# A two-part sequence kernel: constant tables and a channel kernel loaded early, a 127-partition load split, and a second inverse transform in full width

## The chip, the cores and the metric

The kernel runs on one core of one Trainium2 chip. The metric is device time in microseconds (us) of one execution. Engines are called as in the profile: PE (matmul), PEld (weight load), DVE (VectorE), ACT (ScalarE), POOL (GpSimd), SP (SyncE, which here only issues transfers). A suffix q, as in SPq, is the sequencer of an engine. L123 is a line of the kernel in question; the two kernels number their lines differently. "Slow" executions are those that the records mark by a lower granted clock or a time over 1.5% above the fastest of the same kernel; only fast ones are compared. The granted clock is PE's clock as the chip's throttle allowed it, as a share of full speed; the DMA share is the mean busy share of the 16 engines that carry out the core's transfers.

## The reference

Two heads are computed from separate inputs and concatenated. Head A is a diagonal state-space recurrence over 2048 steps with 640 complex states; head B multiplies a short shifted convolution of k by v, convolves the product along the sequence with a 2048-tap kernel for each channel (by FFT), and gates with q.

```python
# A: x [1, 2048, 640]
Lam_bar = exp(dt * Lam);  B_bar = ((Lam_bar - 1) / Lam)[:, None] * Bmat
h_t = Lam_bar * h_{t-1} + B_bar @ x_t
y_A = 2 * real(h @ Cmat.T) + x * Dskip
# B: q, k, v [1, 2048, 640]
kv  = (sum over t of shift(k, t) * shift_k[:, t]) * v
y_B = q * (causal_conv(kv, ssm_k) + kv * ssm_D)
out = concatenate([y_A, y_B], -1)          # bfloat16
```

## The kernel before

Head A first has a setup: B and C are loaded and transposed on PE, x is transposed by the transfer engines, sine and cosine tables are built on DVE, and C is scaled by complex factors. Then, for 20 tiles, come matmuls with B (`st_bu`), a rotation on DVE (`st_rot_in`), a scan and a rotation back (`st_scan`), and later the projection with C.

Head B has four phases, spread over A's steps: `ker` transforms the convolution kernel, `sig` forms kv on DVE and transforms it, `spec` multiplies the spectra, and `inv` goes back and gates with q. They communicate through scratch tensors in DRAM (`scr_ker`, `scr_sig`, `scr_inv`). Every `scr_inv` tile needs all of `ker` and `sig`, and the `inv` phase needs all of `spec`. A framework lays the tiles out in memory like a stack of pools and decides the order of instructions on each engine; that order is fixed when the program is built, so an engine that waits for one input cannot turn to the next instruction.

The parts that the change touches:

```python
# A's setup: everything here lives in pools that close at its end ... [cut]
for src, nm in ((A_C_re, "Cre"), (A_C_im, "Cim")):
    nat[nm] = setup.tile([P, NPT, D], B16, name=f"{nm}_nat")
    nc.sync.dma_start(nat[nm][:], ...)
t1 = setup.tile([P, NPT, NA, NB], F32); t2 = ...        # 2560 elements a partition
nc.vector.tensor_mul(t1[:], bca(CA), bcb(CB))           # six such products in all
...
# B, opened only after A's setup is closed: fp32 tables, staged and cast
with tc.tile_pool(name="b_cstage", bufs=2) as cst:
    self._cast_table(cst, "F1", F1np, self.F1sb, nc.scalar)      # 2 x 1 MB fp32, ACT casts
    ... S2, I2: load, cast;  sk_raw: load, ACT copies into skt
# then the stream pools, then ksb (2.5 MB), in memory that setup or the staging used
...
# sig: the three rows ahead of the tile come from the partition below
nc.sync.dma_start(kh[:, 3 - j0:JC + 3, :], self.k_v[:, 0:j0 + JC, :])
nc.sync.dma_start(kh[1:P, 0:3 - j0, :], self.k_v[0:P - 1, NJ - 3 + j0:NJ, :])   # 127 partitions
...
# spec: the product of half h goes through its own 64-column matmul at once
y_sb = self.sw.tile([P, 512], B16, name="y_sb")
nc.vector.tensor_mul(y_sb[:, 0:cw], pg[:, 0:cw], kt_sb[:, 0:cw])
if h == 0:
    st[("bps", ci)] = self.psum.tile([P, 512], F32, name="bank")
bps = st[("bps", ci)]
nc.tensor.matmul(bps[64*h:64*h+64, lo:hi], lhsT=self.I2sb[:, ..., :], rhs=y_sb[:, lo:hi],
                 start=True, stop=True, tile_position=(0, 64 * h))
if h == 1:
    nc.scalar.copy(Bf[:, c0:c0 + cw], bps[:, 0:cw])
```

## Time and profile before

The median of the first four runs is 366.4 us (363.98 to 368.54). Busy times over the span of 366.8 us:

| engine | busy us | share |
|---|---|---|
| DVE | 281.0 | 77% |
| PE | 237.1 | 65% |
| ACT | 189.8 | 52% |
| POOL | 9.8 | 3% |

I cut the span at three instructions: the first rotation of A (end of setup), the first spectral product y_sb, and the end of the last h_im (end of the spectrum stage). This is the table of busy times by stretch of the kernel before, cut there; the columns are stretch, length, then busy us (and instructions) of PE, PEld, DVE, ACT, POOL, the granted clock, the DMA share and GB/s.

```profile
0.00:48.93 48.93, 15.50 (x120) 12.13 (x120) 34.12 (x92) 25.86 (x46) 4.85 (x10) 0.91 0.65 128
48.93:192.48 143.55, 81.92 (x430) 40.81 (x431) 116.79 (x251) 79.13 (x152) 4.93 (x7) 0.76 0.61 211
192.48:324.29 131.81, 111.09 (x527) 43.06 (x527) 117.38 (x252) 80.09 (x168) 0.00 (x0) 0.95 0.34 117
324.29:366.80 42.51, 28.64 (x204) 17.93 (x202) 12.68 (x25) 4.70 (x12) 0.00 (x0) 0.89 0.77 259
```

Length less DVE's busy time is called DVE's hole in the stage: 26.8 us between setup and spectrum stage, and 14.4 us in the spectrum stage.

### The profile page before, as it was taken

The numbers are of one execution on the slowest core, as the hardware profiler recorded it, in microseconds if no ns is written. First come the engines' busy times: TensorE is split into PE (matmuls) and PEld (weight loads), VectorE is DVE, ScalarE is ACT, GpSimd is POOL, SyncE is SP. The second block draws the span as 40 slices with busy tenths as digits, with TensorE's granted clock in tenths as the row PEclk, the third lists the DMA queues.
The fourth block names the chain that finished last, engine by engine and source line by source line (L and its number), as shares of the span: only waits on it lengthen the run. The fifth ranks groups of instructions, "written<-read, shape, count | busy, mean of one in ns | idle before, by whom it ended". The sixth has DMA issues, their size and how long they took to land.

```text
span 366.8 us, 4211 instructions
## 1 busy us (share of the span) xinstructions
PE 237.1 (65%) x1279; PEld 113.9 (31%) x1279; DVE 281.0 (77%) x616; ACT 189.8 (52%) x377; POOL 9.8 (3%) x17
## 2 busy tenths in 40 slices
PE   2309100680468665673978878879988979786963
PEld 2207000530133222341632424232422424254532
DVE  0399998250589999999999999998898795933333
ACT  1188704770569674565546464747567574730000
POOL 5000020200000000000000000000000000000000
PEclk9999655687559986985898999998989998999888
DMA  7992059440569978853503333333344433147995
GB/s 218 119 236 109 0 170 385 160 160 28 209 183 362 327 243 301 273 184 106 183 32 108 127 108 126 112 122 113 121 155 138 157 109 126 37 165 224 324 324 182
DMA packets 42966, 62.93 MB, mean 172 GB/s; under 512 B 13090, under 2 KB 32161, under 8 KB 42432
## 3 DMA queue, kind: packets, MB, share of 16 engines
q1 hardware_dynamic: 30864, 40.76, 37.7%
q10 hardware_dynamic: 11552, 20.45, 14.5%
q0 software_dynamic: 528, 1.45, 1.5%
q8 instruction: 10, 0.16, 0.2%
q14 instruction: 12, 0.10, 0.1%
HBM read 39.06 MB, written 20.97 MB: 164 GB/s over the span
## 4 chain that ended last, share of the span: by engine, by line
DVE 45%; PE 22%; DMA 20%; issue 5%; SPq 4%; ACT 3%; POOL 1%; DVEq 0%; ACTq 0%; POOLq 0%
DMA in<-in_B_k_dram 6%; PE bank L600 6%; DVE y_sb L595 5%; DMA out_dram<-o 5%; DVE w L535 5%; PE bank L581 5%; DVE g_im L361 4%; DMA cstage<-b_F_d 4%; PE bank L582 3%; DVE g_re L360 3%; DMA dsk_raw<-in_A_Dskip_dram 3%; SPq L517 3%; PE bank L389 2%; DVE o L647 2%; PE bank L321 2%
## 5 line engine op out<-in xcount | busy, mean ns | idle before, releaser
L588 ACT CAST kt_sb<-bank 128x512 bf16<-128x512 f32 (+1 forms) x96 | 47.5, 521 | 22.0 <-PE bank L581 21.2
L595 DVE TENSOR_TENSOR y_sb<-bank,kt_sb 128x512 bf16<-128x512 f32 (+1 forms) x96 | 54.0, 594 | 5.7 <-ACT kt_sb L588 3.1
L490 ACT CAST o<-bank 128x512 bf16<-128x512 f32 x64 | 36.2, 602 | 34.3 <-PE bank L488 13.4
L600 PE MATMUL bank<-y_sb,b_I 128*64 128x512 bf16 (+2 forms) x97 | 34.3, 382 | 23.3 <-DVE y_sb L595 22.6
L389 PE MATMUL bank<-CtRe,h_re 128*128 128x320 bf16 x160 | 48.2, 319 | 0.0
L391 PE MATMUL bank<-CtImN,h_im 128*128 128x320 bf16 x160 | 47.7, 317 | 0.0
L535 DVE TENSOR_TENSOR w<-in,skt 128x1280 bf16<-128x1280 bf16 x32 | 25.2, 815 | 25.9 <-DMA in<-in_B_k_dram 25.9
L402 ACT CAST o_sb<-bank 128x320 bf16<-128x320 f32 x32 | 13.6, 426 | 55.2 <-PE bank L398 55.2
L581 PE MATMUL bank<-in,b_S 128*128 128x512 bf16 (+2 forms) x97 | 35.0, 362 | 0.0
L582 PE MATMUL bank<-in,b_S 128*128 128x512 bf16 (+2 forms) x97 | 34.4, 356 | 0.0
L647 DVE TENSOR_TENSOR o<-bank,in 128x512 bf16<-128x512 f32 x16 | 10.3, 683 | 26.6 <-DMA out_dram<-o 19.2
L603 ACT CAST o<-bank 128x512 bf16<-128x512 f32 (+1 forms) x48 | 24.7, 516 | 9.8 <-PE bank L600 9.2
L321 PE MATMUL bank<-xT,BreT 128*128 128x512 bf16 x100 | 29.4, 431 | 0.2
L488 PE MATMUL bank<-w,b_F 128*128 128x512 bf16 x32 | 14.0, 491 | 21.1 <-DVE w L541 18.6
L323 PE MATMUL bank<-xT,BimT 128*128 128x512 bf16 x100 | 26.1, 393 | 0.0
L504 PE MATMUL bank<-identb,ksb 128*128 128x128 bf16 x80 | 6.6, 248 | 29.1 <-POOL ksb L476 29.1
L581 PEld LDWEIGHTS <-b_S 128*128 128x128 bf16 x97 | 9.4, 97 | 43.1 <-issue 38.5
L488 PE MATMUL bank<-in,b_F 128*128 128x512 bf16 x32 | 12.8, 437 | 11.8 <-ACT o L490 10.2
L389 PEld LDWEIGHTS <-h_re 128*128 128x128 bf16 x160 | 16.7, 104 | 10.1 <-issue 3.6
L360 DVE TENSOR_TENSOR_SCAN g_re<-r,carry_re,mA 128x512 bf16<-128x512 f32 x15 | 19.1, 1274 | 0.0
L361 DVE TENSOR_TENSOR_SCAN g_im<-r,carry_im,mC 128x512 bf16<-128x512 f32 x15 | 19.0, 1269 | 0.0
L391 PEld LDWEIGHTS <-h_im 128*128 128x128 bf16 x160 | 16.6, 104 | 6.7 <-issue 0.5
(161 smaller groups left out, 420.3 us busy)
## 6 DMA issues: line engine op xcount, KB each, us to landing
scr_ker<-o ACTq DMA_DIRECT2D x16, 320.0 KB, 5.3
scr_sig<-o ACTq DMA_DIRECT2D x16, 320.0 KB, 3.1
in<-scr_ker SPq DMA_DIRECT2D x16, 320.0 KB, 2.8
in<-scr_sig SPq DMA_DIRECT2D x16, 320.0 KB, 3.4
scr_inv<-o ACTq DMA_DIRECT2D x16, 320.0 KB, 2.7
in<-scr_inv SPq DMA_DIRECT2D x16, 320.0 KB, 5.6
in<-in_B_k_dram SPq DMA_DIRECT2D x6, 800.0 KB, 6.2
ksb<-in_B_ssm_k_dram SPq DMA_DIRECT2D x1, 2560.0 KB, 17.6
```

Source lines behind the costliest of these rows:

```text
L321: nc.tensor.matmul(a_ps[:, 0:T], lhsT=self.BreT[:, kt, psl], rhs=self.xT[:, kt, tsl], start=(kt == 0), stop=(kt == NPT - 1))
L360: nc.vector.tensor_tensor_scan(g_re[:], rb, u_re[:], init_re, op0=ALU.mult, op1=ALU.add)
L361: nc.vector.tensor_tensor_scan(g_im[:], rb, u_im[:], init_im, op0=ALU.mult, op1=ALU.add)
L389: nc.tensor.matmul(o_ap, lhsT=h_re[:, pt, tt * P:(tt + 1) * P], rhs=self.CtRe[:, pt, half * H:(half + 1) * H], start=first, stop=False)
L391: nc.tensor.matmul(o_ap, lhsT=h_im[:, pt, tt * P:(tt + 1) * P], rhs=self.CtImN[:, pt, half * H:(half + 1) * H], start=False, stop=False)
L490: nc.scalar.copy(a2[:, u, 0:W0], main[:, 0:W0])
L535: nc.vector.tensor_mul(t[:], kh[:, 3 - i:JC + 3 - i, :], skb(i))
L581: nc.tensor.matmul(pk[:, lo:hi], lhsT=self.S2sb[:, 5 if sp else 2 + h, :], rhs=A1["ker"][:, c0 + lo:c0 + hi], start=True, stop=True)
L582: nc.tensor.matmul(pg[:, lo:hi], lhsT=self.S2sb[:, 4 if sp else 0 + h, :], rhs=A1["sig"][:, c0 + lo:c0 + hi], start=True, stop=True)
L588: nc.scalar.copy(kt_sb[:, 0:cw], st[x][0][:, 0:cw])
L595: nc.vector.tensor_mul(y_sb[:, 0:cw], pg[:, 0:cw], kt_sb[:, 0:cw])
L600: nc.tensor.matmul(bps[64 * h:64 * h + 64, lo:hi], lhsT=self.I2sb[:, 1 if sp else 0, :], rhs=y_sb[:, lo:hi], start=True, stop=True, tile_p ...
```

## The change

Its intent is to get the start-up out of the way. Tables come as bf16 and go straight to where they stay; tables and ksb get memory of their own, apart from setup's, so that their loads can start at once; to make room, setup uses less memory (two rotating buffers for B and C, the sine tables by state tile). The 127-partition load is split into 112 and 15. The second inverse transform becomes two accumulating matmuls of 128 columns, both issued after the second half's product.

```diff
@@ A's setup
-                nat[nm] = setup.tile([P, NPT, D], B16, name=f"{nm}_nat")
+                nat[nm] = natp.tile([P, NPT, D], B16, name="nat")      # natp: bufs=2
...              # C is loaded inside pe_transpose, still on nc.sync
-            t1 = setup.tile(shp, F32, name="tab_t1"); ...              # [P, NPT, NA, NB], 6 products
+            for pt in range(NPT):                                      # [P, NA, NB], 30 products
+                t1 = tmp.tile(shp, F32, name="tab_t1"); ...
@@ B's tables: no staging, no cast
-            self._cast_table(cst, "F1", F1np, self.F1sb, nc.scalar)
+        for nm, arr, dst, eng in (("F1", F1np, self.F1sb, nc.scalar), ("S2", ..., nc.gpsimd), ("I2", ..., nc.gpsimd)):
+            self._load_table(nm, arr, dst, eng)                        # one load into dst
@@ ksb
-        knat = ctx.enter_context(tc.tile_pool(name="bk_nat", bufs=1))
+        knat = self.const
@@ sig
-            nc.sync.dma_start(kh[1:P, 0:3 - j0, :], self.k_v[0:P - 1, NJ - 3 + j0:NJ, :])
+            nc.sync.dma_start(kh[1:113, 0:3 - j0, :], self.k_v[0:112, NJ - 3 + j0:NJ, :])
+            nc.sync.dma_start(kh[113:P, 0:3 - j0, :], self.k_v[112:P - 1, NJ - 3 + j0:NJ, :])
@@ spec
-            y_sb = self.sw.tile([P, 512], B16, name="y_sb")
+            y_sb = self.sw.tile([P, 512], B16, name=f"y_sb{h}")
             if h == 0:
-                st[("bps", ci)] = self.psum.tile([P, 512], F32, name="bank")
...
+                st[("y0", ci)] = y_sb
+                return
+            bps = self.psum.tile([P, 512], F32, name="bank")
+            nc.tensor.matmul(bps[:, lo:hi], lhsT=self.I2sb[:, ..., :], rhs=y0[:, lo:hi], start=True, stop=False)
+            nc.tensor.matmul(bps[:, lo:hi], lhsT=self.I2sb[:, ..., :], rhs=y_sb[:, lo:hi], start=False, stop=True)
@@ main: constants of B are allocated before A's setup runs, stream pools after it
```

More of the change, by code (lines that the diff above doesn't have):

```diff
@@ L133, in _sbuf_tables @@
     Minv, Minv0 = _is2_tables()
-    I2bd = np.zeros((128, 2, 64))
-    for gi in range(2):
-        rs = slice(64 * gi, 64 * gi + 64); cs = slice(32 * gi, 32 * gi + 32)
-        I2bd[rs, 0, cs] = Minv
-        I2bd[rs, 1, cs] = Minv0 if gi == 0 else Minv
+    I2bd = np.zeros((128, 2, 2, 128))
+    for v in range(2):
+        for h in range(2):
+            for gi in range(2):
+                g = 2 * h + gi
+                rs = slice(64 * gi, 64 * gi + 64); cs = slice(32 * g, 32 * g + 32)
+                I2bd[rs, v, h, cs] = Minv0 if (v == 1 and g == 0) else Minv
+    I2bd = I2bd.reshape(128, 4, 128)
     return F1sb, G1sb, S2bd.astype(np.float32).astype(bf16), I2bd.astype(np.float32).astype(bf16)
@@ L191, in __init__, with setup @@
         self.sinT = const.tile([P, NPT, T], B16, name="sinT")
+        self.identb = const.tile([P, P], B16, name="identb")
+        self.carry_re = [None] * NPT
+        self.carry_im = [None] * NPT
+        self.pending = {}; self.pend_ab = {}; self.h_cur = None; self.h_done = {}
+        self._args = (x, A_Lambda_re, A_Lambda_im, A_B_re, A_B_im, A_C_re, A_C_im, A_log_dt, A_Dskip, const, prm)
+    def setup(self):
+        tc = self.tc; nc = self.nc; psum = self.psum
+        T = self.T; L = self.L; D = self.D; NPT = self.NPT
+        x, A_Lambda_re, A_Lambda_im, A_B_re, A_B_im, A_C_re, A_C_im, A_log_dt, A_Dskip, const, prm = self._args
+        xT, BreT, BimT = self.xT, self.BreT, self.BimT
         with ExitStack() as sctx:
@@ L195, in __init__ @@
             tmp = sctx.enter_context(tc.tile_pool(name="a_tmp", bufs=2))
+            natp = sctx.enter_context(tc.tile_pool(name="a_nat", bufs=2))
             ident_d = nc.inline_tensor(np.eye(P, dtype=np.float32), name="a_ident")
@@ L198, in __init__ @@
             nc.gpsimd.dma_start(ident[:], ident_d.ap())
-            self.identb = identb = const.tile([P, P], B16, name="identb")
+            identb = self.identb
             nc.vector.tensor_copy(identb[:], ident[:])
@@ L206, in __init__ @@
                 nc.sync.dma_start_transpose(out=xT[:, kt, :], in_=x[:, kt * P:(kt + 1) * P])
-            for src, nm in ((A_C_re, "Cre"), (A_C_im, "Cim")):
-                nat[nm] = setup.tile([P, NPT, D], B16, name=f"{nm}_nat")
-                nc.sync.dma_start(nat[nm][:], src.rearrange("(t p) n -> p t n", p=P))
+            c_srcs = {"Cre": A_C_re, "Cim": A_C_im}
             CreT = setup.tile([P, NPT, D], B16, name="CreT")
@@ L213, in pe_transpose @@
             def pe_transpose(nm, dst):
+                if nm not in nat:
+                    nat[nm] = natp.tile([P, NPT, D], B16, name="nat")
+                    nc.sync.dma_start(nat[nm][:], c_srcs[nm].rearrange("(t p) n -> p t n", p=P))
                 for ct in range(NPT):
@@ L280, in __init__, with bca, bcb @@
                           SB[:].rearrange("p t b -> p (t b)"), CB[:].rearrange("p t b -> p (t b)"), "tabB")
-            shp = [P, NPT, NA, NB]
-            def bca(t):
-                return t[:].unsqueeze(3).to_broadcast(shp)
-            def bcb(t):
-                return t[:].unsqueeze(2).to_broadcast(shp)
+            shp = [P, NA, NB]
             cos4 = self.cosT[:].rearrange("p t (a b) -> p t a b", b=NB)
             sin4 = self.sinT[:].rearrange("p t (a b) -> p t a b", b=NB)
-            t1 = setup.tile(shp, F32, name="tab_t1"); t2 = setup.tile(shp, F32, name="tab_t2")
-            nc.vector.tensor_mul(t1[:], bca(CA), bcb(CB))
-            nc.vector.tensor_mul(t2[:], bca(SA), bcb(SB))
-            nc.vector.tensor_sub(cos4, t1[:], t2[:])
-            nc.vector.tensor_mul(t1[:], bca(SA), bcb(CB))
-            nc.vector.tensor_mul(t2[:], bca(CA), bcb(SB))
-            nc.vector.tensor_add(sin4, t1[:], t2[:])
+            for pt in range(NPT):
+                def bca(t):
+                    return t[:, pt, :].unsqueeze(2).to_broadcast(shp)
+                def bcb(t):
+                    return t[:, pt, :].unsqueeze(1).to_broadcast(shp)
+                t1 = tmp.tile(shp, F32, name="tab_t1"); t2 = tmp.tile(shp, F32, name="tab_t2")
+                nc.vector.tensor_mul(t1[:], bca(CA), bcb(CB))
+                nc.vector.tensor_mul(t2[:], bca(SA), bcb(SB))
+                nc.vector.tensor_sub(cos4[:, pt], t1[:], t2[:])
+                t3 = tmp.tile(shp, F32, name="tab_t1"); t4 = tmp.tile(shp, F32, name="tab_t2")
+                nc.vector.tensor_mul(t3[:], bca(SA), bcb(CB))
+                nc.vector.tensor_mul(t4[:], bca(CA), bcb(SB))
+                nc.vector.tensor_add(sin4[:, pt], t3[:], t4[:])
             pe_transpose("Bre", BreT)
@@ L308, in __init__ @@
                 nc.vector.tensor_scalar_mul(self.Ddiag[:, kt, :], ident[:], dsk[:, kt:kt + 1])
-        self.carry_re = [None] * NPT
-        self.carry_im = [None] * NPT
-        self.pending = {}; self.pend_ab = {}; self.h_cur = None; self.h_done = {}
     def st_bu(self, ck, pt):
@@ L406, with __init__ @@
 class _PartB:
-    def __init__(self, ctx, tc, psum, identb, B_q, B_k, B_v, B_shift_k, B_ssm_k, B_ssm_D, out):
+    def __init__(self, ctx, tc, psum, B_q, B_k, B_v, B_shift_k, B_ssm_k, B_ssm_D, out):
         self.tc = tc; self.nc = tc.nc
@@ L414, in __init__ @@
         self.psum = psum
-        self.identb = identb
-        self.B_ssm_k = B_ssm_k; self.B_ssm_D = B_ssm_D
+        self.identb = None
+        self.B_ssm_k = B_ssm_k; self.B_ssm_D = B_ssm_D; self.B_shift_k = B_shift_k
         self.const = const = ctx.enter_context(tc.tile_pool(name="b_const", bufs=1))
         self.dram = dram = ctx.enter_context(tc.tile_pool(name="b_dram", bufs=1, space=bass.MemoryType.DRAM))
-        F1np, G1np, S2np, I2np = _sbuf_tables(np.float32)
+        F1np, G1np, S2np, I2np = _sbuf_tables(ml_dtypes.bfloat16)
         self.F1sb = const.tile([P, NJ, 2, P], B16, name="b_F1")
@@ L423, in __init__ @@
         self.S2sb = const.tile([P, 6, P], B16, name="b_S2")
-        self.I2sb = const.tile([P, 2, 64], B16, name="b_I2")
+        self.I2sb = const.tile([P, 4, P], B16, name="b_I2")
         self.skt = const.tile([P, 4, D], B16, name="skt")
-        self._G1np = G1np
-        with tc.tile_pool(name="b_cstage", bufs=2) as cst:
-            self._cast_table(cst, "F1", F1np, self.F1sb, nc.scalar)
-            for nm, arr, dst in (("S2", S2np, self.S2sb), ("I2", I2np, self.I2sb)):
-                d = nc.inline_tensor(arr.reshape(P, -1), name=f"b_{nm}_d")
-                st = cst.tile([P, arr.reshape(P, -1).shape[1]], F32, name=f"cstage_{nm}")
-                nc.gpsimd.dma_start(st[:], d.ap())
-                nc.scalar.copy(dst[:].rearrange("p a b -> p (a b)"), st[:])
-            sk_raw = cst.tile([P, D * 4], B16, name="sk_raw")
-            nc.gpsimd.dma_start(sk_raw[:], B_shift_k.rearrange("d k -> (d k)").partition_broadcast(P))
-            nc.scalar.copy(self.skt[:], sk_raw[:].rearrange("p (d k) -> p k d", k=4))
+        self._G1np = G1np; self._tabs = (F1np, S2np, I2np)
         self.scr = {w: dram.tile([32, P, D], B16, name=f"scr_{w}") for w in ("sig", "ker", "inv")}
@@ L442, in __init__, with emit_tables, _load_table @@
         self.out_v = out[0].rearrange("(p j) e -> p j e", j=NJ)
-    def _cast_table(self, pool, nm, arr, dst, eng):
-        nc = self.nc
-        d = nc.inline_tensor(arr.reshape(P, -1), name=f"b_{nm}_d")
-        dflat = dst[:].rearrange("p a b c -> p (a b c)")
-        w = arr.reshape(P, -1).shape[1] // 2
-        for hh in range(2):
-            st = pool.tile([P, w], F32, name="cstage")
-            eng.dma_start(st[:], d.ap()[:, hh * w:(hh + 1) * w])
-            nc.scalar.copy(dflat[:, hh * w:(hh + 1) * w], st[:])
+    def emit_tables(self):
+        tc = self.tc; nc = self.nc; D = self.D
+        F1np, S2np, I2np = self._tabs
+        B_shift_k = self.B_shift_k
+        for nm, arr, dst, eng in (("F1", F1np, self.F1sb, nc.scalar), ("S2", S2np, self.S2sb, nc.gpsimd), ("I2", I2np, self.I2sb, nc.gpsimd)):
+            self._load_table(nm, arr, dst, eng)
+        sk_raw = self.const.tile([P, D * 4], B16, name="sk_raw")
+        nc.gpsimd.dma_start(sk_raw[:], B_shift_k.rearrange("d k -> (d k)").partition_broadcast(P))
+        nc.scalar.copy(self.skt[:], sk_raw[:].rearrange("p (d k) -> p k d", k=4))
+    def _load_table(self, nm, arr, dst, eng):
+        nc = self.nc
+        d = nc.inline_tensor(np.ascontiguousarray(arr.reshape(P, -1)), name=f"b_{nm}_d")
+        pat = "p a b c -> p (a b c)" if len(dst.shape) == 4 else "p a b -> p (a b)"
+        eng.dma_start(dst[:].rearrange(pat), d.ap())
     def load_g1(self):
-        with self.tc.tile_pool(name="b_g1stage", bufs=2) as cst:
-            self._cast_table(cst, "G1", self._G1np, self.G1sb, self.nc.sync)
+        self._load_table("G1", self._G1np, self.G1sb, self.nc.sync)
     def _scr_s1_view(self, which):
@@ L469, in open_ker, with ker_load @@
         NDT = D // P
-        knat = ctx.enter_context(tc.tile_pool(name="bk_nat", bufs=1))
+        knat = self.const
         self.ksb = knat.tile([P, NDT, L], B16, name="ksb")
+        self._dD = knat.tile([P, NDT], B16, name="ssmD")
+    def ker_load(self):
+        nc = self.nc
+        dD = self._dD
         nc.sync.dma_start(self.ksb[:], self.B_ssm_k.rearrange("(t p) n -> p t n", p=P))
-        dD = knat.tile([P, NDT], B16, name="ssmD")
         with nc.allow_non_contiguous_dma("tiny per-channel vector"):
@@ L593, in product_is2 @@
             pk, pg, kt_sb, _ = st.pop(x)
-            y_sb = self.sw.tile([P, 512], B16, name="y_sb")
+            y_sb = self.sw.tile([P, 512], B16, name=f"y_sb{h}")
             nc.vector.tensor_mul(y_sb[:, 0:cw], pg[:, 0:cw], kt_sb[:, 0:cw])
             if h == 0:
-                st[("bps", ci)] = self.psum.tile([P, 512], F32, name="bank")
-            bps = st[("bps", ci)]
-            for lo, hi, sp in segs_for(h, c0, cw):
-                nc.tensor.matmul(bps[64 * h:64 * h + 64, lo:hi], lhsT=self.I2sb[:, 1 if sp else 0, :], rhs=y_sb[:, lo:hi],
-                                 start=True, stop=True, tile_position=(0, 64 * h))
-            if h == 1:
-                nc.scalar.copy(Bf[:, c0:c0 + cw], st.pop(("bps", ci))[:, 0:cw])
+                st[("y0", ci)] = y_sb
+                return
+            y0 = st.pop(("y0", ci))
+            bps = self.psum.tile([P, 512], F32, name="bank")
+            for lo, hi, sp in segs_for(0, c0, cw):
+                nc.tensor.matmul(bps[:, lo:hi], lhsT=self.I2sb[:, 2 * (1 if sp else 0) + 0, :], rhs=y0[:, lo:hi], start=True, stop=False)
+                nc.tensor.matmul(bps[:, lo:hi], lhsT=self.I2sb[:, 2 * (1 if sp else 0) + 1, :], rhs=y_sb[:, lo:hi], start=False, stop=True)
+            nc.scalar.copy(Bf[:, c0:c0 + cw], bps[:, 0:cw])
         n = len(subs)
@@ L674 @@
     pa = _PartA(ctx, tc, psum, A_x, A_Lambda_re, A_Lambda_im, A_B_re, A_B_im, A_C_re, A_C_im, A_log_dt, A_Dskip, out)
-    pb = _PartB(ctx, tc, psum, pa.identb, B_q, B_k, B_v, B_shift_k, B_ssm_k, B_ssm_D, out)
+    pb = _PartB(ctx, tc, psum, B_q, B_k, B_v, B_shift_k, B_ssm_k, B_ssm_D, out)
+    pb.identb = pa.identb
+    kctx = ExitStack()
+    pb.open_ker(kctx)
+    pa.setup()
+    pb.emit_tables()
+    pb.ker_load()
+    bctx = ctx.enter_context(ExitStack())
+    pb.open_stream(bctx)
     NG = NJ // JC
@@ L680 @@
     NU = len(units)
-    bctx = ctx.enter_context(ExitStack())
-    pb.open_stream(bctx)
-    kctx = ExitStack()
-    pb.open_ker(kctx)
     last_ker = max(i for i, (ph, _) in enumerate(units) if ph == "ker")
```

## The prediction

> **What bounds the kernel now.** I read the page's strip first, then a table of busy times by stage, which I cut where the strip changes character: 0 to 49 us is setup, 49 to 102 the loading of tables and first inputs, 102 to 190 the kernel and signal stages, 190 to 323 the spectrum stage, 323 to the end the inverse stage. The columns are: stretch, its length, then busy time (instructions) of PE, PEld, DVE, ACT and POOL, the granted clock, DMA share and GB/s.
>
> ```profile
> 0.00:16.00 16.00, 4.87 (x43) 4.55 (x44) 1.46 (x9) 2.07 (x3) 4.85 (x10) 1.00 1.01 159
> 16.00:24.30 8.30, 1.12 (x10) 0.69 (x7) 8.09 (x67) 6.62 (x17) 0.00 (x0) 1.00 1.19 216
> 24.30:49.00 24.70, 9.51 (x70) 6.89 (x70) 24.63 (x18) 17.17 (x27) 0.00 (x0) 0.82 0.23 77
> 49.00:62.00 13.00, 0.00 (x0) 0.00 (x0) 12.98 (x36) 1.90 (x1) 2.47 (x4) 0.50 0.92 347
> 62.00:102.00 40.00, 19.41 (x109) 10.12 (x110) 13.40 (x28) 20.49 (x34) 2.46 (x3) 0.67 0.41 143
> 102.00:190.00 88.00, 62.51 (x321) 30.70 (x321) 87.86 (x178) 56.09 (x116) 0.00 (x0) 0.83 0.68 228
> 190.00:323.00 133.00, 109.80 (x516) 42.08 (x516) 118.60 (x258) 80.34 (x169) 0.00 (x0) 0.95 0.34 114
> 323.00:366.80 43.80, 29.93 (x216) 18.92 (x213) 13.94 (x28) 5.11 (x12) 0.00 (x0) 0.89 0.76 255
> ```
>
> The third figure after the length is what matters. DVE is full from 16 to 62 us and again from 102 to 190, and 89% busy in the spectrum stage. So from 16 to 323 us the time is DVE's work plus DVE's holes, and a change pays only where it closes a hole. There are two: 40.00 - 13.40 = 26.6 us between 62 and 102, and 133.00 - 118.60 = 14.4 us in the spectrum stage. The inverse stage is another matter: DVE has 13.94 us of work in 43.8, and what it waits for there is output and scratch transfers.
>
> The first hole is explained by the timeline of DVE and of the SP issue queue (start, length, what):
>
> ```profile
> 62.01 0.43 DVE L378 TENSOR_TENSOR h_im<-nA,nB 128x512 bf16<-128x512 bf16 x1
> 70.63 0.82 DVE L535 TENSOR_TENSOR w<-in,skt 128x1280 bf16<-128x1280 bf16 x1 [8.20 <-DMA in<-in_B_k_dram]
> 91.35 0.83 DVE L535 TENSOR_TENSOR w<-in,skt 128x1280 bf16<-128x1280 bf16 x1 [12.73 <-DMA in<-in_B_k_dram]
> 101.92 0.83 DVE L535 TENSOR_TENSOR w<-in,skt 128x1280 bf16<-128x1280 bf16 x1 [5.00 <-DMA in<-in_B_k_dram]
> ...
> 49.04 0.37 SPq L472 DMA_DIRECT2D ksb<-in_B_ssm_k_dram  x1
> 67.59 0.34 SPq L517 DMA_DIRECT2D in<-in_B_k_dram  x1
> 67.98 0.33 SPq L518 DMA_DIRECT2D in<-in_B_k_dram  x1
> ...
> 79.34 1.77 SPq L518 DMA_DIRECT2D in<-in_B_k_dram  x1
> ```
>
> All three holes, 25.9 us, end on a load of k. The first load is issued only at 67.59, just after ACT's copy into skt ends: its buffer lies where the staging tiles of the tables were, and these lie where setup was, which is free at 49. The later two wait for line 518, which loads partitions 1 to 127. The DMA view of 79 to 103 us shows it:
>
> ```profile
> DMA  9968951000000000000001939400989896000000
> GB/s 384 241 166 286 414 192 55 28 26 26 26 26 26 26 26 32 26 26 26 23 26 55 405 130 388 173 28 26 122 335 437 356 471 218 23 26 23 28 28 32
> ```
>
> For long stretches 26 GB/s flow, where 380 to 470 are possible: one engine of 16 works.
>
> **What the Trainium skill says.** "DMA: Bandwidth & Descriptors", section on why a DMA increments its semaphore by 16, says that the slowest dimension decides how many engines share a transfer: the largest divisor up to 16, and it lists 127 partitions as going to one. Its Specifications give some 27 GiB/s per engine. The trace agrees (26 GB/s). By that rule the new pieces of 112 and 15 partitions use 16 and 15 engines, which no run yet shows. "VectorE: DVE Perf Modes", section "Mode 2x_2P", says that fp32 tensor_tensor stays at 1x; at the page's 0.96 GHz 2560 elements are 2.67 us, and the trace has 2.82 for L289 to L294, so about 0.15 is fixed. "TensorEngine Tiling (Array Packing)", Key Properties and Restrictions, says that changing the tiling mode drains the engine and that column tiling loses fast weight load. The 64-column weight loads of L600 took 110 ns against 97 for the full ones of L581, and its 128x512 matmuls 417 against 394, so there is little to win there.
>
> **The change part by part.**
> (1) The split of the 127-partition load. Two loads go through one engine, 476.2 and 158.8 KB; 650 thousand bytes at 26 GB/s are 25 us. On 15 or 16 engines they are 2 to 3 us. With this the 12.73 and 5.00 us waits should go: -17.7.
> (2) Tables in bf16, straight into place, in memory that setup does not touch; ksb too. Before, from 49 us: two 1 MB pieces of F1 and ksb's 2.56 MB queue up, ACT casts F1 (2 x 1.90), S2 (0.83), I2 (0.29) and copies skt (2.48); ksb's correction is at 66.7 and the k load at 67.59. After, all these loads depend on nothing and should be issued within setup. The k load waits only for setup's memory: about 52 in place of 67.6. DVE meanwhile has 13 us of A's rotation and scan, so the data (5 to 8 us after issue) is there in time: -8.2. The casts themselves lie on ACT, which is not the bound: 0. The same holds of G1's two casts.
> With the small waits on ACT at 71 to 73 us (0.7) these make up the 26.6. I keep 3.5 us of it, as the first kernel units run beside a just-waking PE (clock 0.5) and several loads start together.
> (3) The sine tables by state tile: six products of 2560 elements (2.74 to 2.86 us apart, 16.9 in all) become 30 of 512. Each is 512/0.96 = 0.53 us plus 0.07 to 0.15, say 0.63: 18.9 us. On the full DVE: +2.0.
> (4) Early traffic. F1 (1.05 MB), skt's source (0.66), S2 and I2 (0.33) now share 0 to 24 us with the transposes of x, where the DMA share is already 1.0. 2 MB at some 370 GB/s are 5.5 us of all engines. What DVE waits for at 11 to 16 us are tiny vectors on another queue; and C, behind ksb perhaps, has slack until the tables end. I charge +2.0 of the 5.5.
> (5) The second inverse transform as two accumulating 128x128 matmuls in place of two 128x64 ones. Their number and length on PE are equal. What goes is a wait: PE stood 22.6 us before L600 for y_sb, in order, and so held up the next products' matmuls. Half of the L600 stops vanish, and the bank is taken later. But DVE is what bounds most of this stage: from 190 to 241 it idles under 2 us. Only the 14.4 us of holes, mostly after 258, can shrink. I take a third: -5.0.
> (6) The inverse stage loses nothing: same transfers. 0.
> Sum: 366.4 - 26.6 + 3.5 + 2.0 + 2.0 - 5.0 = 342.3 us.
>
> **Rivals.** (a) Setup becomes later. If the early loads push the tiny vectors or, with ksb's 2.56 MB ahead of C (7 us), the C transposes beyond the tables' end at about 44 us, DVE starves and everything shifts by 4 to 8 us: 347 to 350. For it: DMA at 1.0 from 6 us on; the small C pool now makes C's loads wait for B's transposes, so ksb may well go first. Against: CtRe's first step came at 38.2 and tables then still had 3 us to run, so there is slack. (b) The bound moves to the transfers: in 102 to 190 the DMA share is 0.68, and the same bytes now fall in a shorter time with the scratch writes of 320 KB beside them; then only some 15 us of the hole close: about 352. Against: F1 and ksb, 4.6 MB of fp32 and kernel data, leave that stretch. (c) All closes, and PE, unblocked, runs ahead through the spectrum stage so that DVE is full there as well: 366.4 - 26.6 - 12 + 4 = 332. For it: PE has 109.8 us of work in 133. Against: ACT and PE have other waits of their own (DVE for A's evacuated products, 7.3 us in this stage). (d) Nothing gained because the waits were hidden: this the trace rules out nearly, since all three stops are DVE's own and it has no slack from 102 to 190.
>
> **Range and chances.** (a) and (b) make the upper end, 352; (c) the lower, 332, a little lower if little of the 3.5 us stays: 331. The two halves of the hole are separate mechanisms and one alone gives over 2%, so faster: 0.95; within 2%: 0.04; slower: 0.01.
>
> **What would show it.** Right: no SP stretch at 26 GB/s; the first k load issued between 49 and 56 us; F1, S2 and I2 loads before 25 us and no casts of b_F; DVE's holes between setup's end and the spectrum stage under 6 us in all; table products near 0.63 us apart; PE's wait for y_sb before the new inverse matmuls about 11 us; the inverse stage again 44 us. Wrong: k loads still gated past 60 us; DVE holes in 24 to 50 us on C or the tables; waits for scratch writes in the kernel stage; or a spectrum stage as long as before. A time above 352 would mean that the hole moved, not closed.

## The result

The changed kernel takes 334.72 us (median of 11 runs, 333.17 to 338.95, the last of which is slow), the kernel before 366.29 (16 runs). The ratio is 0.9139, with a 95% interval of 0.9108 to 0.9170. Ratios here are those for the fast runs of the same rounds, close to the ratio of the medians quoted but not quite the same. The range of 331 to 352 us holds it, and so does the forecast "faster"; the centre was 7.6 us too high.

The same table of stretches for the changed kernel, cut at the same instructions:

```profile
0.00:51.00 51.00, 18.49 (x160) 14.13 (x161) 36.32 (x116) 27.73 (x47) 8.14 (x15) 0.99 0.83 235
51.00:166.90 115.90, 78.56 (x392) 37.98 (x392) 115.90 (x251) 68.09 (x145) 2.26 (x2) 0.78 0.57 193
166.90:292.36 125.46, 101.14 (x516) 49.11 (x516) 115.09 (x252) 79.51 (x167) 0.00 (x0) 0.95 0.36 121
292.36:332.80 40.44, 27.82 (x214) 17.69 (x212) 12.67 (x24) 5.12 (x12) 0.00 (x0) 0.96 0.81 276
```

Row by row against before: setup +2.07, kernel and signal stages -27.65, spectrum stage -6.35, inverse stage -2.07; together -34.0, the difference of the two spans. The medians differ by 31.6 only: the profiled execution of the kernel before took 368.54 us, 2.3 above its median, so the rows together overstate the gain by 2.4 us. In the second row DVE's busy time equals the length: the hole of 26.8 us is gone to the last tenth. The DVE instructions there are the same 251.

Why it is gone, on SP's issue queue of the changed kernel (start, length of the issue):

```profile
28.83 0.52 SPq L484 DMA_DIRECT2D ksb<-in_B_ssm_k_dram  x1
51.11 0.34 SPq L528 DMA_DIRECT2D in<-in_B_k_dram  x1
51.50 0.42 SPq L529 DMA_DIRECT2D in<-in_B_k_dram  x1
```

ksb now starts at 28.83 us, 20 us earlier, and the first k load at 51.11, just after setup's last DVE instruction at 50.20 to 51.08; before it was 67.59. And on DVE's timeline of the same kernel:

```profile
77.28 0.81 DVE L547 TENSOR_TENSOR w<-in,skt 128x1280 bf16<-128x1280 bf16 x1
```

The first use of k comes at 77.28 us, 26 us after its load was issued, and shows no wait at all. DVE has been through four tiles of A's rotations and scans by then: the order of instructions was built anew as well.

Setup, which got longer, has two opposite movements in it. DVE's timeline before, two lines:

```profile
16.07 0.17 DVE L228 CAST dsk_f<-dsk_raw 128x5 f32<-128x5 bf16 x1 [1.05 <-DMA dsk_raw<-in_A_Dskip_dram]
24.31 2.82 DVE L289 TENSOR_TENSOR tab_t<-tab_CA,tab_CB 128x2560 f32<-128x2560 f32 x1
```

and after:

```profile
12.96 0.17 DVE L243 CAST dsk_f<-dsk_raw 128x5 f32<-128x5 bf16 x1 [0.47 <-DMA dsk_raw<-in_A_Dskip_dram]
21.20 0.68 DVE L305 TENSOR_TENSOR tab_t<-tab_CA,tab_CB 128x512 f32<-128x512 f32 x1
39.02 0.89 DVE L320 SCALAR_TENSOR_TENSOR CtRe<-CimT,ngim,ct_t 128x640 bf16<-128x640 bf16 x1 [0.29 <-ACT CimT L233]
42.12 0.88 DVE L323 SCALAR_TENSOR_TENSOR CtImN<-CimT,ngre,ct_t 128x640 bf16<-128x640 bf16 x1 [1.62 <-ACT ct_t L322]
46.22 0.89 DVE L320 SCALAR_TENSOR_TENSOR CtRe<-CimT,ngim,ct_t 128x640 bf16<-128x640 bf16 x1 [1.62 <-ACT ct_t L319]
```

The last tiny vector arrives 3.1 us earlier, and with it the first table product moves from 24.31 to 21.20. But from there to setup's end DVE takes 29.8 us in place of 24.6, and 0.29 + 1.62 + 1.62 = 3.5 us of that are waits for ACT's work on C, which arrives later: it is issued at 27.71 us after the transposes of x, where before it was 23.67.

In the spectrum stage, three groups of the page before (line, engine, operation, count | busy us, mean ns | idle before, and whom for):

```profile
L588 ACT CAST kt_sb<-bank 128x512 bf16<-128x512 f32 (+1 forms) x96 | 47.5, 521 | 22.0 <-PE bank L581 21.2
L595 DVE TENSOR_TENSOR y_sb<-bank,kt_sb 128x512 bf16<-128x512 f32 (+1 forms) x96 | 54.0, 594 | 5.7 <-ACT kt_sb L588 3.1
L600 PE MATMUL bank<-y_sb,b_I 128*64 128x512 bf16 (+2 forms) x97 | 34.3, 382 | 23.3 <-DVE y_sb L595 22.6
```

and their counterparts after:

```profile
L600 ACT CAST kt_sb<-bank 128x512 bf16<-128x512 f32 (+1 forms) x96 | 47.6, 524 | 12.4 <-DVE y_sb L607 11.3
L607 DVE TENSOR_TENSOR y_sb<-bank,kt_sb 128x512 bf16<-128x512 f32 (+1 forms) x96 | 51.7, 590 | 1.9 <-ACT kt_sb L600 1.1
L614 PE MATMUL bank<-y_sb,b_I 128*128 128x512 bf16 (+3 forms) x49 | 18.1, 370 | 22.0 <-DVE y_sb L607 21.8
L615 PE MATMUL bank<-y_sb,b_I 128*128 128x512 bf16 (+3 forms) x49 | 18.2, 371 | 3.6 <-DVE y_sb L607 3.5
```

PE's wait for y_sb did not shrink: 21.8 + 3.5 = 25.3 us against 22.6. What changed is ACT's line. Before, ACT waited 21.2 us for PE; after, it waits 11.3 us for DVE, that is, for DVE to finish with a buffer that it wants to write again. PE runs ahead with the next products, ACT has them evacuated ahead of time, and DVE is the one waited for. PE does still stop for the first half's product: L614 multiplies it, and 21.8 of the 25.3 us are there. But it stops later. On PE's timeline the longest row of matmuls of the first transform between two of the second is six before (L581 and L582) and eight after (L593 and L594), seven times each. DVE's own idle before y_sb falls from 5.7 to 1.9 us. Of the stage's 6.35 us, 4.1 are hole (14.4 to 10.4 us); the other 2.3 are DVE's busy time (117.38 to 115.09), most of it in y_sb (54.0 to 51.7 us for the same 96 products, where the busy time counts overlapping records once).

### The profile page after: what moved, and what is told of

The parts are those of the page before. It is cut to its first block, busy times and chain, and to the rows that moved or that the text cites. A ratio compares the mean times of both kernels' runs of the same rounds, so it can differ in the third digit from the quotient of the medians.

```text
span 332.8 us, 4194 instructions
## 1 busy us (share of the span) xinstructions
PE 226.0 (68%) x1280; PEld 118.9 (36%) x1280; DVE 280.0 (84%) x640; ACT 180.4 (54%) x371; POOL 10.4 (3%) x17
## 4 chain that ended last, share of the span: by engine, by line
DVE 48%; PE 21%; DMA 9%; SPq 8%; issue 7%; ACT 5%; DVEq 0%; ACTq 0%
DVE y_sb L607 8%; SPq L220 8%; DVE w L547 5%; DMA out_dram<-o 4%; DVE g_re L373 4%; DVE g_im L374 4%; PE bank L402 3%; PE bank L593 3%; PE bank L404 3%; PE bank L615 3%; PE bank L594 3%; PE bank L336 2%; PE bank L334 2%; DVE o L660 2%; DMA nat<-in_A_C_re_dram 2%
## 5 line engine op out<-in xcount | busy, mean ns | idle before, releaser
L600 ACT CAST kt_sb<-bank 128x512 bf16<-128x512 f32 (+1 forms) x96 | 47.6, 524 | 12.4 <-DVE y_sb L607 11.3
L607 DVE TENSOR_TENSOR y_sb<-bank,kt_sb 128x512 bf16<-128x512 f32 (+1 forms) x96 | 51.7, 590 | 1.9 <-ACT kt_sb L600 1.1
L501 ACT CAST o<-bank 128x512 bf16<-128x512 f32 x64 | 36.6, 605 | 30.5 <-PE bank L499 20.8
L402 PE MATMUL bank<-CtRe,h_re 128*128 128x320 bf16 x160 | 48.9, 323 | 0.0
L404 PE MATMUL bank<-CtImN,h_im 128*128 128x320 bf16 x160 | 48.5, 321 | 0.0
L594 PE MATMUL bank<-in,b_S 128*128 128x512 bf16 (+2 forms) x97 | 34.0, 351 | 0.0
L593 PE MATMUL bank<-in,b_S 128*128 128x512 bf16 (+2 forms) x97 | 33.9, 355 | 0.0
L614 PE MATMUL bank<-y_sb,b_I 128*128 128x512 bf16 (+3 forms) x49 | 18.1, 370 | 22.0 <-DVE y_sb L607 21.8
L499 PE MATMUL bank<-w,b_F 128*128 128x512 bf16 x32 | 16.6, 575 | 23.0 <-DVE w L553 22.8
L232 PE MATMUL bank<-identb,nat 128*128 128x128 bf16 x100 | 9.9, 290 | 28.2 <-DMA nat<-in_A_C_re_dram 13.8
L334 PE MATMUL bank<-xT,BreT 128*128 128x512 bf16 x100 | 26.8, 400 | 1.6 <-ACT o L501 1.4
L336 PE MATMUL bank<-xT,BimT 128*128 128x512 bf16 x100 | 25.2, 383 | 0.0
L499 PEld LDWEIGHTS <-b_F 128*128 128x128 bf16 x64 | 7.4, 118 | 39.9 <-DVE w L553 25.9
L615 PE MATMUL bank<-y_sb,b_I 128*128 128x512 bf16 (+3 forms) x49 | 18.2, 371 | 3.6 <-DVE y_sb L607 3.5
L402 PEld LDWEIGHTS <-h_re 128*128 128x128 bf16 x160 | 16.9, 106 | 8.5 <-issue 2.0
L232 PEld LDWEIGHTS <-nat 128*128 128x128 bf16 x100 | 9.2, 136 | 28.7 <-DMA nat<-in_A_C_re_dram 14.1
```

What stands on the lines that cost most here:

```text
L334: nc.tensor.matmul(a_ps[:, 0:T], lhsT=self.BreT[:, kt, psl], rhs=self.xT[:, kt, tsl], start=(kt == 0), stop=(kt == NPT - 1))
L336: nc.tensor.matmul(b_ps[:, 0:T], lhsT=self.BimT[:, kt, psl], rhs=self.xT[:, kt, tsl], start=(kt == 0), stop=(kt == NPT - 1))
L402: nc.tensor.matmul(o_ap, lhsT=h_re[:, pt, tt * P:(tt + 1) * P], rhs=self.CtRe[:, pt, half * H:(half + 1) * H], start=first, stop=False)
L404: nc.tensor.matmul(o_ap, lhsT=h_im[:, pt, tt * P:(tt + 1) * P], rhs=self.CtImN[:, pt, half * H:(half + 1) * H], start=False, stop=False)
L501: nc.scalar.copy(a2[:, u, 0:W0], main[:, 0:W0])
L593: nc.tensor.matmul(pk[:, lo:hi], lhsT=self.S2sb[:, 5 if sp else 2 + h, :], rhs=A1["ker"][:, c0 + lo:c0 + hi], start=True, stop=True)
```

## The experiments

Twelve kernels ran, each correct. The "before" of their ratios is the kernel before, run between them on the same chip (medians of 365.3 to 365.8 us). They ran in three groups, each in rounds of its own: e1, e2, e3, e6; e4, e5, e8, e9; e7, e10, e11, e12. The changed kernel itself was in none of these rounds, so it can be set against them by ratios only. The stage lengths of their profiles, cut as above, with DVE's hole in the second stage:

| kernel | setup | kernel+signal (hole) | spectrum | inverse | median us | ratio |
|---|---|---|---|---|---|---|
| before | 48.9 | 143.6 (26.8) | 131.8 | 42.5 | 366.3 | 1 |
| changed | 51.0 | 115.9 (0.0) | 125.5 | 40.4 | 334.7 | 0.914 |
| e1 before + split | 48.2 | 125.5 (8.9) | 132.2 | 40.8 | 348.9 | 0.954 |
| e2 changed - split | 51.0 | 123.0 (7.0) | 124.5 | 41.8 | 342.7 | 0.937 |
| e6 changed - split - transform | 50.8 | 123.4 (7.4) | 129.9 | 41.1 | 348.9 | 0.953 |
| e3 changed - transform | 50.6 | 115.9 (0.0) | 128.6 | 41.3 | 339.9 | 0.930 |
| e4 old transform, more buffers | 50.8 | 115.9 (0.0) | 132.2 | 41.7 | 340.5 | 0.932 |
| e5 deferred, 64 columns | 49.8 | 115.9 (0.0) | 127.3 | 41.7 | 336.8 | 0.922 |
| e7 before + transform | 47.8 | 144.0 (27.3) | 126.6 | 42.9 | 362.4 | 0.992 |
| e8 large table products | 41.1 | 126.8 (0.0) | 124.6 | 43.5 | 335.6 | 0.920 |
| e9 F1 behind x | 51.0 | 118.3 (2.1) | 127.0 | 43.6 | 338.6 | 0.924 |
| e10 C by POOL | 48.4 | 115.9 (0.0) | 125.5 | 41.1 | 333.0 | 0.913 |
| e11 e10 + large products | 49.7 | 114.0 (0.0) | 127.0 | 41.0 | 333.9 | 0.913 |
| e12 unsplit, by POOL | 50.5 | 115.9 (0.0) | 124.8 | 42.1 | 335.6 | 0.918 |

In e8 and e11 another order of instructions moves the cut between the first two stages, so only their sum can be compared. The profile of e9 fell in a slow execution. The inverse stage lies between 40.4 and 43.6 us whatever was changed, so its 2.07 us in the result are within the spread of single profiles, and I give them no cause.

### The split and the early loads: are they two halves?

e1 is the kernel before with nothing but the split:

```diff
-            nc.sync.dma_start(kh[1:P, 0:3 - j0, :], self.k_v[0:P - 1, NJ - 3 + j0:NJ, :])
+            nc.sync.dma_start(kh[1:113, 0:3 - j0, :], self.k_v[0:112, NJ - 3 + j0:NJ, :])
+            nc.sync.dma_start(kh[113:P, 0:3 - j0, :], self.k_v[112:P - 1, NJ - 3 + j0:NJ, :])
```

> The kernel before with the 127-partition load split into 112 and 15 and nothing else. Theory T (two separate halves of the hole): the waits of 12.7 and 5.0 us go, the first of 8.2 us stays, 366.3 - 17.7 = about 349 us. Rival R (the late tables and ksb hold the stage anyway, so that another wait takes the place): over 356 us.

348.85 us (3 rounds), a ratio of 0.954: theory T to the microsecond. Of the three k waits on DVE's timeline only the first is left:

```profile
70.02 0.82 DVE L536 TENSOR_TENSOR w<-in,skt 128x1280 bf16<-128x1280 bf16 x1 [8.28 <-DMA in<-in_B_k_dram]
```

e2 is the changed kernel with that split taken back, the reverse of the diff above.

> The changed kernel with the one load of 127 partitions put back. T (separate halves): 334.7 + 17.7 = about 352 us. Rival R (overlap): the changed kernel issues these loads at 51.5 us and DVE asks for the first of them only at 77.3 us; 0.65 MB at 26 GB/s are 25 us, so the slow transfer ends about when it is first needed, and the time is 335 to 340 us.

342.65 us (5 rounds), between the two theories. The split is worth 17 us in the kernel before and 8 in the changed one. The way in which it still costs 8 us is neither theory's. The DMA view of e2 from 51 to 79 us shows the single engine at work (second line GB/s, slices of 0.7 us):

```profile
DMA  0673100029003804984979410000000000004700
GB/s 0 62 271 135 34 27 27 22 112 379 31 27 152 335 27 197 337 246 196 157 210 411 192 57 35 22 27 27 22 27 27 22 27 27 22 26 172 318 24 24
```

and yet DVE has no wait for k. Its one large wait in the stage is this:

```profile
76.77 0.42 DVE L350 TENSOR_TENSOR mB<-sinT,b 128x512 bf16<-128x512 bf16 x1 [6.56 <-ACT b L340]
```

It waits for ACT, which in turn stood for 13.4 us, as ACT's timeline shows:

```profile
61.05 0.33 ACTq L503 DMA_DIRECT2D scr_ker<-o  x1
75.78 0.33 ACTq L503 DMA_DIRECT2D scr_ker<-o  x1
76.15 0.58 ACT L340 CAST b<-bank 128x512 bf16<-128x512 f32 x1 [13.38 <-DMA in<-in_B_k_dram]
```

ACT issues the scratch writes of the kernel phase in line with its other work. Between 61.05 and 75.78 us no write was issued, while the load of k went through one engine; SP's own issues of v in this run lasted 10.12 and 13.53 us. So the slow load reaches DVE by a detour, through a scratch write of another queue that could not be issued, and an evacuation behind it. The kernel before has the same stop beside its own slow load: no scratch write between 78.20 and 91.33 us, and ACT waits 10.96 us there. In the changed kernel no such stop is left; up to 79.36 us its scratch writes follow each other within 4 us. How the one queue holds the other up no run shows.

e6 leaves only the early loads: split and transform are both as before.

> The changed kernel with the split and the new second inverse transform both undone: only tables and ksb early (with the sine tables by state tile). T: the 8.2 us wait goes, setup is 2.1 us longer: 366.3 - 8.2 + 2.1 = about 360 us. R: early loading alone closes most of the hole, and the time is that of the unsplit run plus the 6.4 us of the spectrum stage, 342 to 346 us.

348.88 us. T is wrong by 11 us, and R's range is 3 us too low, as it was in e2. DVE's one large wait is again the detour: 6.9 us for ACT's evacuation, which stands 13.76 us. With e1, e3 and the kernel before, all in the same rounds, this makes a square, all with the old transform:

| | 127 partitions in one | split |
|---|---|---|
| tables and ksb late | 365.8 | 348.9 |
| tables and ksb early | 348.9 | 339.9 |

Either alone saves 16.9 us, both together 25.9: about 8 us can be had from either and only once. The holes say it more clearly, without setup's 2 us: 26.8 with neither, 8.9 with the split, 7.4 with the early loads, 0.0 with both. Early loading does not only take away the first wait of 8.2 us. It also lets the k load start 16 us earlier, ahead of its use, so that most of the slow transfer lies beside A's rotations and scans. The early loads are one bundle here, together with the bf16 tables, the new memory layout and the order of instructions that follows from it; which part of the bundle is needed was not tested.

e12 tests whether the number of engines is the cause, without touching the shape of the load:

```diff
-            nc.sync.dma_start(kh[1:P, 0:3 - j0, :], self.k_v[0:P - 1, NJ - 3 + j0:NJ, :])
+            nc.gpsimd.dma_start(kh[1:P, 0:3 - j0, :], self.k_v[0:P - 1, NJ - 3 + j0:NJ, :])
```

> The changed kernel with one load of 127 partitions again, but issued from POOL's queue. If the number of engines is what made it slow and software descriptors spread 127 partitions over 16 engines, as the Trainium skill's page on DMA says: no stretch at 26 GB/s and about 335 us. If the odd number of partitions is slow by any queue: 342 us, as with the unsplit load on SP.

335.55 us, a ratio of 0.918 with 0.9151 to 0.9217, against 0.937 on SP: the same 127 partitions in one load cost next to nothing from the other queue (the changed kernel has 0.914, and the intervals overlap). The 476 KB landed 8.2 us after issue, and no stretch at 26 GB/s is left, as the DMA view of 51 to 75 us shows:

```profile
DMA  1789999999997997277670048000940574800480
GB/s 13 98 316 384 444 393 350 341 393 311 265 237 203 367 401 286 81 286 286 262 294 9 21 192 354 0 0 0 371 175 0 230 316 188 358 0 0 188 358 0
```

The Trainium skill ("DMA: Bandwidth & Descriptors", section on why a DMA increments its semaphore by 16) says that software descriptors are an exception and spread some direct copies, of 127 partitions too, over 16 engines; this run agrees.

### The second inverse transform

e3 is the changed kernel with the transform of before (table, tile and matmuls as in the section on the kernel before).

> The changed kernel with the second inverse transform of before (two 64-column matmuls, each issued at once). T: the spectrum stage goes back from 125.5 to 131.8 us, about 341 us in all. Rival: the spectrum stage got shorter because of the scheduler's other order or a better clock, and the time stays at 335 us.

339.93 us (5 rounds), 0.930 against 0.914: 5.7 us by the ratios (0.0156 of 366), with a spectrum stage of 128.6 us. e6 and e2, which differ in the transform alone and ran in the same rounds, give 0.0162, 5.9 us. e7 has only the new transform, in the kernel before.

> The kernel before with nothing but the new second inverse transform. If its gain lies in the spectrum stage alone and does not depend on what comes earlier: 365.7 - 6 = about 360 us with a spectrum stage of 125 to 127 us in place of 131.8; the 26.6 us hole stays. Rival: the stage only gets shorter together with the early loads, and the time stays at 365 us.

362.39 us, a ratio of 0.992 (0.9879 to 0.9955): less than 2%, but the interval leaves out 1. The stage is 126.6 us long, 5.3 less than before, so the gain is there without the early loads. The whole gains 3.0 us; the profile has the inverse and second stages 0.4 and 0.5 us longer, and I can't say whether more than spread is in that.

e4 and e5 take the transform apart. e4 keeps the matmuls of before and changes only the buffers; e5 defers the first half's matmul but keeps 64 columns.

```diff
# e4, against e3
-            y_sb = self.sw.tile([P, 512], B16, name="y_sb")
+            y_sb = self.sw.tile([P, 512], B16, name=f"y_sb{h}")
# e5, against the changed kernel
-                nc.tensor.matmul(bps[:, lo:hi], lhsT=self.I2sb[:, ..0, :], rhs=y0[:, lo:hi], start=True, stop=False)
-                nc.tensor.matmul(bps[:, lo:hi], lhsT=self.I2sb[:, ..1, :], rhs=y_sb[:, lo:hi], start=False, stop=True)
+            for hh, y in ((0, y0), (1, y_sb)):
+                nc.tensor.matmul(bps[64*hh:64*hh+64, lo:hi], lhsT=self.I2sb[:, .., :], rhs=y[:, lo:hi],
+                                 start=True, stop=True, tile_position=(0, 64 * hh))
```

> The changed kernel with the 64-column inverse matmuls issued at once, as before, but with y_sb in two sets of three buffers, as in the changed kernel. Theory D (deferral: PE no longer stops for the first half's y_sb, so it runs ahead with the next products): buffers give nothing, about 340 us as in the run with the old transform. Rival B (buffers): about 335 us.

> The changed kernel with 64-column matmuls kept, but both issued after the second half's y_sb, into a bank taken then: the deferral without the 128-column form. Theory D: all of the gain, about 335 us and a spectrum stage of 125 us. Rival F (the full-width form gains, as no tiling mode is switched and weights load faster): about 340 us.

e4 takes 340.48 us (0.932), no better than e3: the buffers are not it. e5 takes 336.83 (0.922; 0.9195 to 0.9241), in the same rounds as e4: the deferral alone is worth 0.0106 of 366, 3.9 us. That is the larger part. ACT's wait, too, goes over from PE to DVE with the deferral alone; in e4 it is still 16.1 us for PE, and e5's page has

```profile
L597 ACT CAST kt_sb<-bank 128x512 bf16<-128x512 f32 (+1 forms) x96 | 47.1, 523 | 10.7 <-DVE y_sb L604 9.5
```

The longest row of first-transform matmuls is eight in e5 as well. What is left for the full width lies between 0.8 us (e5 against e8, which has the full-width transform, in the same rounds) and 2.9 us (e5 against the changed kernel, in other rounds); whether there is a gain from the width at all, these runs don't settle. In these profiles the stage's length also goes with the granted clock: with the old transform it was 132.2 us at 0.94 (e1, e4), 131.8 at 0.95 (before), 129.9 at 0.97 (e6) and 128.6 at 0.99 (e3).

### The start of setup

e9 issues F1's load from SP, behind the transposes of x, in place of ACT's queue at the start:

```diff
-        for ... in (("F1", F1np, self.F1sb, nc.scalar), ...
+        for ... in (("F1", F1np, self.F1sb, nc.sync), ...
```

> The changed kernel with F1's load moved from ACT's queue to SP's, behind the transposes of x. Theory V (F1's megabyte at the start slows B, so the transposes start later and the tiny vectors land ahead of them): without it the vectors land at 16 us again in place of 13, the first table product starts at 24.3 us in place of 21.2, the transposes end near 24 us; setup ends 1 to 3 us later, 335 to 338 us. Rival (the vectors land earlier for another reason): the first product stays at 21.2 us.

DVE's timeline of e9:

```profile
16.71 0.17 DVE L243 CAST dsk_f<-dsk_raw 128x5 f32<-128x5 bf16 x1 [2.50 <-DMA dsk_raw<-in_A_Dskip_dram]
24.95 0.68 DVE L305 TENSOR_TENSOR tab_t<-tab_CA,tab_CB 128x512 f32<-128x512 f32 x1
```

So it is F1's load at 0.75 us that brings the vectors in 3 to 4 us earlier, odd as that is: the megabyte delays the loads of B (they land 10.8 and 15.9 us after issue in the changed kernel, 4.7 and 9.2 in e9). That this delays the transposes behind B, and so leaves the vectors room, is my reading of the queues, and was not tested. This profile fell in a slow execution, but the fast ones agree: the last vector is in at 15.0 to 16.1 us in the three kernels that load F1 late (before, e1, e7), and at 12.6 to 14.1 in all that load it first. Those have their first table product at 20.8 to 22.6 us. The theory was wrong in two points. The transposes still hold SP to 27.5 us, so it isn't F1 that delays C. And setup ends at 50.97 us, as in the changed kernel: when the tables start late, DVE's waits for C between 25 and 51 us vanish, and the early start of the changed kernel had been spent in waiting for C. The median is 338.57 us (0.924), 3.9 us above the changed kernel; its profile shows 2.1 us of that as a DVE hole at 61 us on ACT's evacuation, which I did not follow further.

e8 undoes the sine tables by state tile (six products of 2560 elements, in a pool of their own that closes after them).

> The changed kernel with the sine tables in six products of 2560 elements again. Theory T: DVE work falls by 18.1 - 16.9 = 1.2 us on the full engine, about 333.5 us. Rival C (the C tables hold setup's end, since DVE already waits for ACT there): setup ends at 51 us as before and the time stays at 334.7 us.

335.59 us (5 rounds): no gain, as the rival had it, though by another way. The new order puts A's first rotation in front of the C tables, and there DVE waits 5.8 us at 41 us for the evacuation of A's first matmul. Setup and the second stage together take 167.9 us, against 166.9.

e10 takes the loads of C out of SP's queue, and e11 adds the large products:

```diff
-                    nc.sync.dma_start(nat[nm][:], c_srcs[nm].rearrange("(t p) n -> p t n", p=P))
+                    nc.gpsimd.dma_start(nat[nm][:], c_srcs[nm].rearrange("(t p) n -> p t n", p=P))
```

> The changed kernel with the two loads of C issued from POOL's queue, so that they need not stand behind the transposes of x on SP. Theory C (DVE's 3.5 us of waits at 38 to 46 us come from C's late arrival at 34 us): C lands near 20 to 25 us, the waits go, setup ends near 47.5 us, about 331 us. Rival X (the shared engines are full of transposes anyway and x's arrival bounds, or C's traffic delays x): setup ends at 50 to 51 us and the time is 334 to 336 us.

> As the run before, with the sine tables in six large products again. Theory C: with C early, DVE's work alone bounds setup, so the 1.2 us that gave nothing alone now count: about 330 us. Rival: as with the large products alone, the scheduler puts A's first rotation ahead of the C tables and DVE waits for x: 334 to 336 us.

POOL's timeline of e10 has the issues of C at 14.93 and 21.04 us in place of 27.71 and 28.31:

```profile
14.93 0.87 POOL L228 DMA_DIRECT2D nat<-in_A_C_re_dram  x1 [5.20 <-PE bank L232]
21.04 0.86 POOL L228 DMA_DIRECT2D nat<-in_A_C_im_dram  x1 [5.23 <-PE bank L232]
```

The 3.5 us of waits are gone from DVE's timeline, and setup ends at 48.35 us in place of 51.00. e10 takes 333.01 us (331.51 to 335.69) and e11 333.86. The ratio of 0.9126 (0.9086 to 0.9165) can't be told from the changed kernel's 0.9139; the profile's stages show the 2.65 us in setup. The transposes of x, for their part, now hold SP for 30.25 us in place of 25.76, as rival X had it, but nothing waits for that. So e10 is the fastest median, and very likely not slower, but an advantage over the changed kernel is not shown. e11 gives nothing on top.

## Why the prediction was right, step by step

**Right: what bounds.** The reading that DVE's work plus its holes make up the time from 16 to 323 us held: DVE has 280.0 us of work after, 281.0 before, and the gain is holes.

**(1) and (2), the hole of 26.6 us: sum right, division wrong.** The two k waits were charged to the split (-17.7) and the first wait to the early loads (-8.2), as "separate mechanisms". For the split alone this is exact (e1: 366.3 - 17.7 = 348.6 predicted, 348.85 measured). For the early loads it is not: alone they close 26.8 - 7.4 = 19.4 us of the hole (e6). The step that failed is the assumption that the early loads only take away the wait for the first load. They start the slow load as a whole 16 us earlier, ahead of its use, and so take over about half of what the split saves: 17.9 us of hole with the loads late, 7.4 with them early. The sum came out right because the hole was counted once. The sentence that one alone gives over 2% was true of each. One figure was set beside another unit: 27 GiB/s, the page's rate of an engine, are 29 GB/s, so the trace's 26 GB/s are a tenth lower. How many engines carried the pieces of 112 and 15 partitions, no view shows; no stretch at 26 GB/s is left.

**The 3.5 us kept back.** Nothing was left of the hole. PE's low clock and the crowd of loads did not reach DVE, since the new order gives DVE A's work until 77 us.

**(3) the sine tables, +2.0.** The 30 products started 0.60 us apart, 18.1 us in all. The prediction's 16.9 for the six is the sum of their records, of 2.82 us each, which overlap; from start to start they take 16.7, so +1.4. Of the fixed part of 0.15 us, half lies beside the next product: 0.60 - 0.53 = 0.07 counts. Taking this work away again gained nothing in e8, though in another order of instructions.

**(4) early traffic, +2.0.** Wrong in both parts, nearly right in sum. The vectors came 3.1 us earlier, not later (e9 shows F1 to be the cause), and C came 4 us later and cost 3.5 us (e10 shows that). Setup grew by 2.1 us where (3) and (4) had 4.0, so that the two came so near is luck.

**(5) the spectrum stage, -5.0.** -6.35 in the profile, 5.7 us by the ratio of e3. It took a third of the hole; measured are 4.1 us of hole and 2.3 of DVE's busy time, which it did not have. That the first half's matmul is put off is the larger part (e4, e5). The sign named for it, PE's wait for y_sb down to some 11 us, was wrong, and so was "half of the L600 stops vanish": the wait stayed, and ACT's 21.2 us wait for PE went.

**(6) the inverse stage, 0.** The spread of the profiles covers what was measured.

Of the signs named for "right", all but that one came: no stretch at 26 GB/s, the k load at 51.11 us, the tables issued from 0.75 to 6.4 us, no hole before the spectrum stage, products 0.60 us apart. Of those for "wrong", DVE's waits for C in 24 to 50 us came too, 3.5 us.

Of the rivals, (a) came true in kind, as C did starve DVE, and not in size. (b), a stage bound by transfers, did not: no DVE hole is left there. (c) was close in time, though it has all of the spectrum stage's holes closed and in fact 125.46 - 115.09 = 10.4 us remain, 7.9 of them before the rotations of A.

By terms: the centre missed by 7.6 us. 3.5 are the part of the hole kept back, 1.9 setup, 1.35 the spectrum stage. The 0.8 left over is less than the spread of single profiles, from which these terms are read. The lower end of 331 was put below (c) for the 3.5 us, though (c) keeps none of them.

## What to carry to other kernels

Look for transfers whose partition count lets them run on few engines, as 127 did here, and for buffers that share memory with something earlier: the first show as long stretches at the rate of a single engine, the second as loads that are issued late without any need. Two such faults in front of the same consumer are not two gains to be added: a load that starts early enough hides part of its slowness (here about half of 17 us), so test each alone and both together. And when a queue is shared, follow the slow load to the other queues; here it reached the bound engine by way of a scratch write that had nothing to do with it.

## What the Trainium skill lacked or had wrong

- "DMA: Bandwidth & Descriptors" says that 127 partitions from SP or ACT use one engine, and more from POOL; both agree (26 GB/s; 476 KB in 8.2 us by POOL). For Trainium2 it doesn't say what such a load does to others (the nearest is a remark on the next chip, that one issuing processor no longer blocks another there): ACT's scratch writes were not issued for 14.7 us beside it (e2), and v's issues on SP lasted 10.1 and 13.5 us.
- The same page, section "Issuing engines are not separate DMA queues", calls the sequencer's time to issue "usually small relative to the DMA itself". Here is an exception: five transposes of x held SP for 21.8 us before and 25.8 after, about as long as they moved data (DMA share 1.0 and more over the first 24 us before), and the loads of C stood behind them; issued from POOL they started at 14.9 us in place of 27.7 (e10).
- No page says that a large load on one queue can bring tiny ones on another in earlier: 12.96 against 16.07 us, and 16.71 with the large load moved away (e9). Why it does so, no run shows in full.
- "TensorEngine Tiling (Array Packing)", Key Properties, gives the drain at a change of tiling mode without a size. Between 64 and 128 columns for 98 matmuls the runs have 0.8 to 2.9 us, not settled.
